# Reordering the prologue of a spectral-filter and MLP kernel: warm-up matmuls, first table group, filter loads and last product pair

## The chip, the cores and the metric

The kernel runs on one core of one Trainium2 chip. The metric is device microseconds of one execution, smaller is better. The profile's "span" is the time from the first to the last instruction of one profiled execution; the measured time was 2.1 to 2.2 us longer than the span of the same execution in runs of the kernel before. Engines are written TensorE (PE in profile lines), VectorE (DVE), ScalarE (ACT), GpSimd (POOL) and SyncE (SP). L107 is line 107 of that kernel's source, so the same statement has another number in another version.

Unless it is called a single look, a result below is six runs in the fast state, of which one was profiled. A single look is one run, whose state is unknown.

## The reference

```python
# x (8, 3008, 256), filt_r and filt_i (1505, 256), w_in (256, 2048), w_out (2048, 256), beta (2048)
X = np.fft.rfft(x, axis=1)
y = np.fft.irfft(X * (filt_r + 1j * filt_i)[None], n=3008, axis=1)   # the mixing
t = y.reshape(8 * 3008, 256)
h = t @ w_in
g = h * (1.0 / (1.0 + np.exp(-beta * h)))
out = g @ w_out
```

The kernel computes the transforms as matmuls with sine and cosine tables that it makes on the chip, in a 47 x 64 factorization.

## The kernel before

The first batch item's mixing has to be finished before the MLP can start, and nothing else can fill TensorE meanwhile. This is the prologue. From then on the MLP loop runs, and the mixing of the other seven items is woven into it. The prologue's steps are:

1. Load x of item 0 in six transfers and make the tables: the first in `t1b`, the second, `t2`, from angles `u` and `r` on VectorE (first half) and GpSimd (second half), a sine on ScalarE, and three copies (`t2_more`).
2. First stage (`first1`, eight groups), evicted to `a_t`.
3. Turns: `a_t` transposed into `a2`.
4. Twelve products: second-stage matmuls, evicted by VectorE with a multiplication by the filter `fri`, two per product (`pb_t`, `qb_t`).
5. The inverse (`inverse3`) with tables `t3`, `t3b`, which are transposes of `t2` (`table3`), to `z_t`; then turns of z, the last stage to `y`, and the loop.

The filters come in three groups, `FG`: products 1 to 3 use group 0, products 4 to 6 use group 1, and products 7 to 12 use group 2. The "lower" half of a filter is in long rows, the "upper" half in 1 KB rows. `held` is a tiny GpSimd read that keeps the large loads of `w_in`, `w_out` and the next x back until group 1's upper halves are there.

```python
    mark = dpool.tile([1, D], BF16, name="mark", tag="mark")
    nc.sync.dma_start(mark[:], x_cur[:1, JG, :])       # SyncE's queue waits here for x's third transfer
    ...
    FG = ((0, KG), (KG, KG), (2 * KG, 2 * KG))
    for h in range(2):
        for f, at in ((filt_r, 0), (filt_i, M)):
            load_filter(fri, f, at, *FG[0], gp)[h]()                 # group 0: GpSimd
    for h in (1, 0):
        for f, at in ((filt_r, 0), (filt_i, M)):
            load_filter(fri, f, at, *FG[1], nc.sync)[h]()            # group 1: SyncE
    for go in load_filter(fri, filt_r, 0, *FG[2], nc.sync):          # group 2, real part: SyncE
        go()
    ...
    warm(12)                                    # 12 matmuls on zeros, their result is not used
    ...                                         # angles, tables
    held = setup.tile([P, 1], F32, name="held", tag="held")
    for p0 in (H, M + H):
        gp.tensor_copy(held[p0 : p0 + H], fri[p0 : p0 + H, 2 * KG - 1, :1])
    load_win(0); load_win(1); load_wout(0) ...  # GpSimd's large loads, behind held (shortened)
    for i in range(2):
        first1(i, (True, True))
        warm(2)
    t2_part(0, 0)
    first1(2, (False, False))
    warm(2)
    for part in (1, 2):
        t2_part(0, part)
    for go in load_filter(fri, filt_i, M, *FG[2], nc.scalar):        # group 2, imaginary part: ScalarE
        go()
    for i in range(3, 5):
        first1(i, (False, False))
        warm(2)
    t2_more(0, nc.vector)                       # three table copies on VectorE
    first1(5, (True, True))
    ...
    turn_a(0, False)
    turn_a(1, True)
    ...
    table3(0, 2, True)
    product(0)
    table3(0, 0, False)                         # first table group, evicted between the products
    FLAG = 2
    for i in range(NK // 2 + FLAG):
        if 0 < i < NK // 2:
            product(i)
        ...                                     # further turns and table groups
        if i >= FLAG:
            inverse3(i - FLAG)
    for i in range(4):
        scale_wout(i)
    for at in (0, M):                           # frr, for the later items: SyncE's queue
        for go in load_filter(frr, filt_r, at, 0, JG, nc.sync):
            go()
```

## Time and profile before

Three runs before the prediction gave a median of 790.13 us (790.11 to 791.49). The execution that was profiled was a fourth one and took 792.89 us, with a span of 790.8 us. The mean granted TensorE clock of that execution was 0.997.

| what | value |
|---|---|
| time, median of 3 | 790.13 us |
| time and span of the profiled execution | 792.89 us, 790.8 us |
| first product on VectorE | 19.70 us |
| seventh product | 29.52 us |
| first matmul of the loop | 41.36 us |
| granted TensorE clock, 10 to 15 us | 0.66 |

From the profile page of before: the busy time of each engine, with its share of the span and its instructions, and the chain of work that ended last, by engine.

```profile
PE 772.1 (98%) x6001; PEld 548.0 (69%) x6097; DVE 395.7 (50%) x643; ACT 596.9 (75%) x920; POOL 144.6 (18%) x143
...
PE 92%; DVE 3%; issue 2%; POOL 2%; ACT 1%; DVEq 0%; ACTq 0%; POOLq 0%
```

The loop is TensorE's. The prologue is not, so its own timeline must be read. From the timeline of VectorE, before; the columns are start and duration in us, engine, line, operation, output and input, count, and in brackets the idle time before it and what ended that.

```profile
13.38 0.35 DVE L289 TENSOR_SCALAR t<-t 128x768 bf16<-128x768 bf16 x1
13.65 0.98 DVE L290 COPY t<-t 128x768 bf16<-128x768 bf16 x1
14.55 1.97 DVE L291 COPY t<-t 128x768 bf16<-128x768 bf16 x1
16.45 0.54 DVE L107 CAST a_t<-psa 128x384 bf16<-128x384 f32 x1
17.63 0.56 DVE L107 COPY a<-pb 128x768 bf16<-128x768 bf16 x1 [0.64 <-PE pb L409]
19.70 0.69 DVE L442 TENSOR_TENSOR pb_t<-ps,fri 128x512 bf16<-128x512 f32 x1 [1.52 <-DMA fri<-in_filt_i_dram]
...
29.52 0.68 DVE L442 TENSOR_TENSOR pb_t<-ps,fri 128x512 bf16<-128x512 f32 x1
```

The three copies (the first with a change of sign) are of one size and take 0.35, 0.98 and 1.97 us. The first product (19.70) was released by a filter's landing. The seventh (29.52) waited for nothing, and VectorE has no gap between the two: in this execution VectorE is what limits the products.

From the timeline of TensorE, the first matmul of the loop:

```profile
41.36 1.02 PE L791 MATMUL hps<-y,win_sb 128*128 128x512 bf16 x4 [0.35 <-DVE y L109]
```

### The profile page before, as it was taken

The numbers are of one execution on the slowest core, as the hardware profiler recorded it, in microseconds if no ns is written. First come the engines' busy times: TensorE is split into PE (matmuls) and PEld (weight loads), VectorE is DVE, ScalarE is ACT, GpSimd is POOL, SyncE is SP. The second block draws the span as 40 slices with busy tenths as digits, with TensorE's granted clock in tenths as the row PEclk, the third lists the DMA queues.
The fourth block names the chain that finished last, engine by engine and source line by source line (L and its number), as shares of the span: only waits on it lengthen the run. The fifth ranks groups of instructions, "written<-read, shape, count | busy, mean of one in ns | idle before, by whom it ended". The sixth has DMA issues, their size and how long they took to land.

```text
span 790.8 us, 15274 instructions
## 1 busy us (share of the span) xinstructions
PE 772.1 (98%) x6001; PEld 548.0 (69%) x6097; DVE 395.7 (50%) x643; ACT 596.9 (75%) x920; POOL 144.6 (18%) x143
## 2 busy tenths in 40 slices
PE   7899999999999999999999999999999999999998
PEld 4767667766677667776668766687667766776665
DVE  7946935755527464465634746367462760500101
ACT  5887886886678866788667876778767788677776
POOL 8421510430014200131002310024100340000000
PEclk9999999999999999999999999999999999999999
DMA  8978678116811178011860229402370214010101
GB/s 183 235 191 215 145 207 224 56 67 187 204 56 47 68 200 218 29 68 60 216 190 28 78 103 197 155 30 92 126 208 27 74 68 127 28 54 27 55 27 53
DMA packets 83379, 91.43 MB, mean 116 GB/s; under 512 B 3758, under 2 KB 73536, under 8 KB 82286
## 3 DMA queue, kind: packets, MB, share of 16 engines
q1 hardware_dynamic: 79756, 73.16, 30.0%
q0 software_dynamic: 2816, 16.26, 10.8%
q10 hardware_dynamic: 736, 1.05, 0.6%
q8 instruction: 47, 0.77, 0.4%
q14 instruction: 24, 0.20, 0.1%
HBM read 57.16 MB, written 46.66 MB: 131 GB/s over the span
## 4 chain that ended last, share of the span: by engine, by line
PE 92%; DVE 3%; issue 2%; POOL 2%; ACT 1%; DVEq 0%; ACTq 0%; POOLq 0%
PE acc L826 42%; PE hps L791 37%; PE ps L599 3%; PE ps L522 3%; PE ps L621 2%; PE ps L647 2%; DVE ost L107 1%; POOL xg L116 0%; POOL r L269 0%; DVE qb_t L442 0%; ACT a L105 0%; DVE pb_t L442 0%; PE pb L409 0%; PE psz L452 0%; DVE q_t L636 0%
## 5 line engine op out<-in xcount | busy, mean ns | idle before, releaser
L800 ACT ACTIVATE gT<-hps,beta_sb 128x512 bf16<-128x512 f32 x752 | 516.5, 687 | 175.8 <-PE hps L791 147.9
L826 PE MATMUL acc<-wout_sb,gT 128*128 128x256 bf16 x3008 | 455.1, 272 | 3.8 <-ACT ost L105 0.2
L791 PE MATMUL hps<-y,win_sb 128*128 128x512 bf16 (+7 forms) x1634 | 427.4, 350 | 0.3 <-DVE y L109 0.3
L826 PEld LDWEIGHTS <-gT 128*128 128x128 bf16 x3008 | 285.4, 98 | 132.6 <-issue 4.5
L791 PEld LDWEIGHTS <-win_sb 128*128 128x128 bf16 x1728 | 164.7, 98 | 24.8 <-issue 0.7
L637 POOL TENSOR_TENSOR v_t<-p_t,q_t 128x512 bf16<-128x512 f32 x84 | 106.7, 1270 | 376.3 <-DVE q_t L636 373.7
L107 DVE COPY ost<-acc 128x512 f32<-128x512 f32 (+1 forms) x88 | 56.2, 677 | 193.6 <-PE acc L826 188.0
L107 DVE CAST a<-ps 96x512 bf16<-96x512 f32 x96 | 65.9, 687 | 85.5 <-PE ps L599 85.4
L109 DVE TENSOR_SCALAR y<-ps 128x376 bf16<-128x376 f32 (+2 forms) x120 | 64.5, 541 | 64.4 <-PE ps L522 64.2
L632 DVE TENSOR_TENSOR p_t<-ps,frr 128x512 f32<-128x512 f32 x84 | 58.1, 691 | 31.8 <-PE ps L621 29.5
L636 DVE TENSOR_TENSOR q_t<-ps,fri 64x512 f32<-64x512 f32 x84 | 58.2, 693 | 1.2
L633 DVE SCALAR_TENSOR_TENSOR q_t<-ps,fri 64x512 f32<-64x512 f32 x84 | 57.4, 684 | 1.1
L522 PEld LDWEIGHTS <-zz 96*128 96x128 bf16 x512 | 35.3, 97 | 29.0
L105 ACT ACTIVATE z<-ps 128x512 bf16<-128x512 f32 x84 | 49.5, 589 | 0.7 <-PE ps L647 0.7
L599 PE MATMUL ps<-xg,t 94*96 94x512 bf16 x112 | 41.9, 381 | 0.8
L522 PE MATMUL ps<-t,zz 96*128 96x94 bf16 x448 | 36.7, 204 | 1.1
L116 POOL DMA_DIRECT2D xg<-in_x_dram x22 | 12.1, 556 | 114.3 <-PE acc L826 97.7
L647 PE MATMUL ps<-v_t,t 128*128 128x256 bf16 x168 | 32.1, 273 | 0.4 <-DVE q_t L636 0.4
L621 PE MATMUL ps<-a,t 128*128 128x256 bf16 x168 | 32.1, 273 | 0.4
L621 PEld LDWEIGHTS <-t 128*128 128x128 bf16 x168 | 15.8, 98 | 14.6
L599 PEld LDWEIGHTS <-t 94*96 94x96 bf16 x112 | 13.8, 123 | 12.1
L647 PEld LDWEIGHTS <-t 128*128 128x128 bf16 x168 | 15.4, 98 | 8.1 <-DVE q_t L636 0.9
(118 smaller groups left out, 196.9 us busy)
## 6 DMA issues: line engine op xcount, KB each, us to landing
out_dram<-ost SPq DMA_DIRECT2D x40, 512.0 KB, 2.8
d<-a SPq DMA_DIRECT2D x28, 384.0 KB, 3.5
a<-d SPq DMA_DIRECT2D x28, 384.0 KB, 5.2
d<-z SPq DMA_DIRECT2D x28, 384.0 KB, 2.6
zz<-d SPq DMA_DIRECT2D x28, 384.0 KB, 4.4
xg<-in_x_dram POOLq DMA_DIRECT2D x6, 1280.0 KB, 10.2
frr<-in_filt_r_dram SPq DMA_DIRECT2D x12, 256.0 KB, 6.8
out_dram<-ost SPq DMA_DIRECT2D x22, 128.0 KB, 9.0
```

What stands on the lines that cost most here:

```text
L107: nc.vector.tensor_copy(dst, src)
L109: nc.vector.tensor_scalar_mul(dst, src, scale)
L522: nc.tensor.matmul(ps[:, e, :NP], lhsT=zz[:, jj + e, dc * P : (dc + 1) * P], rhs=tab[:], start=True, stop=True,)
L599: nc.tensor.matmul(ps[:KP], lhsT=t1[:], rhs=s["x"][:, 2 * i : 2 * i + 2, :], start=True, stop=True)
L621: nc.tensor.matmul(ps[:, e, :], lhsT=t2[:, k0 + e, 3:5, :].rearrange("p c k -> p (c k)"), rhs=s["a2"][g][:, kk + e, :], start=True, stop=True,
L632: nc.vector.tensor_tensor(p_t[:], ps[:], frr[:, ks_, :], ALU.mult)
L636: nc.vector.tensor_tensor(q_t[:M], ps[M:P], fri[M:P, ks_, :], ALU.mult)
L637: nc.gpsimd.tensor_tensor(v_t[:], p_t[:], q_t[:], ALU.add)
L647: nc.tensor.matmul(ps[:, e, :], lhsT=t3[:, k0 + e, :], rhs=v_t[:, e, :], start=True, stop=True)
L791: nc.tensor.matmul(hps[:, pos - t0 : pos - t0 + ln], lhsT=win_sb[:, dc, fb * P : (fb + 1) * P], rhs=ys[b][:, dc, n0 : n0 + ln], start=(dc ...
L800: nc.scalar.activation(gT[:, :tn], hps[:, :tn], ACT.Silu, scale=beta_sb[:, fb : fb + 1])
L826: nc.tensor.matmul(acc[tb // per][:, tb % per, :], lhsT=gT[:, tb * P : (tb + 1) * P], rhs=wout_sb[:, fb, :], start=(fb == 0 and tb % per = ...
```

## The change

Its intent, in four parts:

- **Warm-ups.** More matmuls on zeros ahead of the third first-stage group (14 in place of 12 at the start, 8 in place of 2 later, and 1 in place of 2 before the last group), to keep TensorE's clock up while it waits for x.
- **First table group.** Its transposes are issued right behind the first stage and its evictions come before the first turn, so that they leave the stretch of products.
- **Filters.** Group 2 is loaded wholly on SyncE, in the order in which it is used, and no longer half on ScalarE. The `held` wait and GpSimd's large loads move behind the first stage in the program; some of those loads move to the fourth step.
- **Last pair.** Its two halves go to two PSUM banks and are evicted by ScalarE and VectorE at once.

The diff, cut to its core (cuts marked `...`; the moved code is not shown twice):

```diff
-    for go in load_filter(fri, filt_r, 0, *FG[2], nc.sync):
-        go()
+    for h in (0, 1):
+        for f, at in ((filt_r, 0), (filt_i, M)):
+            load_filter(fri, f, at, *FG[2], nc.sync)[h]()
...
-    warm(12)
+    warm(14)
...
     for i in range(2):
         first1(i, (True, True))
-        warm(2)
+        warm(2 if i == 0 else 8)
...
-    for go in load_filter(fri, filt_i, M, *FG[2], nc.scalar):
-        go()
...
     first1(7, (False, True))
+    tabs = [
+        table3(0, 0, False, fpsum.tile([P, KG, P], BF16, name="pt", tag="f")),
+        table3(0, 2, True, hpsum.tile([P, KG, P], BF16, name="pt", tag="hps")),
+    ]
+    for go in tabs:
+        go()
...
+    for p0 in (H, M + H):
+        gp.tensor_copy(held[p0 : p0 + H], fri[p0 : p0 + H, 2 * KG - 1, :1])
...
     turn_a(0, False)
     turn_a(1, True)
...
+        last = i == NK // 2 - 1
+        one = opsum.tile([P, 2, NDC, P], F32, name="psz", tag="acc")
+        two = fpsum.tile([P, 2, NDC, P], F32, name="psz", tag="f") if last else one
...
-    table3(0, 2, True)
     product(0)
-    table3(0, 0, False)
     FLAG = 2
+    TAB = (1, 2, 5, 6, 8, 9)
```

More of the change, by code (lines that the diff above doesn't have):

```diff
@@ L288, in t2_more @@
         ks_ = slice(h * NH, (h + 1) * NH)
-        eng.tensor_scalar_mul(t2[:, ks_, 4, :], t2[:, ks_, 1, :], -1.0)
+        nc.vector.tensor_scalar_mul(t2[:, ks_, 4, :], t2[:, ks_, 1, :], -1.0)
         eng.tensor_copy(t2[:, ks_, 3, :], t2[:, ks_, 2, :])
@@ L313 @@
     )
-    held = setup.tile([P, 1], F32, name="held", tag="held")
-    for p0 in (H, M + H):
-        gp.tensor_copy(held[p0 : p0 + H], fri[p0 : p0 + H, 2 * KG - 1, :1])
-    def load_win(h):
-        fs = slice(h * FF // 2, (h + 1) * FF // 2)
-        gp.dma_start(win_sb[:, :, fs], moe_w_in[:, fs].rearrange("(dc p) f -> p dc f", p=P))
-    load_win(0)
-    load_win(1)
-    load_wout(0)
-    xs = {}
-    if B > 1:
-        xs[1] = load_x(1, X_HALVES[:2])
-    load_wout(1)
-    if B > 1:
-        load_x(1, X_HALVES[2:], xs[1])
-        mark3 = dpool.tile([1, D], BF16, name="mark3", tag="mark3")
-        nc.sync.dma_start(mark3[:], xs[1][:1, J - 1, :])
-    load_wout(2)
-    load_wout(3)
     a_t = ypool.tile([P, NDC, NK, J, 4], BF16, name="a_t", tag="y")
@@ L367, with table3, go @@
         t2_part(0, part)
-    for go in load_filter(fri, filt_i, M, *FG[2], nc.scalar):
-        go()
+    def table3(i, part, on_act, own=None):
+        pt = own or opsum.tile([P, KG, P], BF16, name="pt", tag="acc")
+        for e in range(KG):
+            nc.tensor.transpose(
+                pt[:, e, :],
+                t2[:, KG * i + e, part : part + 2, :].rearrange("p c k -> p (c k)"),
+                ident[:],
+            )
+        dst = t3 if part else t3b
+        def go():
+            if i > 0:
+                evac(dst[:, KG * i : KG * i + KG, :], pt[:], on_act)
+                return
+            if part:
+                evac(dst[:, 0, :], pt[:, 0, :], on_act, 0.5)
+            else:
+                nc.vector.tensor_scalar_mul(dst[:, 0, :], pt[:, 0, :], keep[:])
+            evac(dst[:, 1:KG, :], pt[:, 1:KG, :], on_act)
+        return go
     for i in range(3, 5):
@@ L376 @@
     first1(6, (True, True))
-    warm(2)
+    warm(1)
     first1(7, (False, True))
-    def table3(i, part, on_act):
-        pt = opsum.tile([P, KG, P], BF16, name="pt", tag="acc")
-        for e in range(KG):
-            nc.tensor.transpose(
-                pt[:, e, :],
-                t2[:, KG * i + e, part : part + 2, :].rearrange("p c k -> p (c k)"),
-                ident[:],
-            )
-        dst = t3 if part else t3b
-        if i == 0:
-            if part:
-                evac(dst[:, 0, :], pt[:, 0, :], on_act, 0.5)
-            else:
-                nc.vector.tensor_scalar_mul(dst[:, 0, :], pt[:, 0, :], keep[:])
-            evac(dst[:, 1:KG, :], pt[:, 1:KG, :], on_act)
-        else:
-            evac(dst[:, KG * i : KG * i + KG, :], pt[:], on_act)
+    tabs = [
[4 more added lines that the diff above has]
+        go()
     a2s = []
@@ L414, in turn_a, with load_win @@
         evac(a2s[-1][:, 3 * (i % 2) : 3 * (i % 2) + 3, :], pb[:], on_act)
+    held = setup.tile([P, 1], F32, name="held", tag="held")
+    for p0 in (H, M + H):
+        gp.tensor_copy(held[p0 : p0 + H], fri[p0 : p0 + H, 2 * KG - 1, :1])
+    def load_win(h):
+        fs = slice(h * FF // 2, (h + 1) * FF // 2)
+        gp.dma_start(win_sb[:, :, fs], moe_w_in[:, fs].rearrange("(dc p) f -> p dc f", p=P))
+    load_win(0)
+    load_win(1)
+    load_wout(0)
+    xs = {}
+    if B > 1:
+        xs[1] = load_x(1, X_HALVES[:2])
     turn_a(0, False)
@@ L447, in inverse3 @@
         p_t, q_t = pq.pop(i)
-        ps = opsum.tile([P, 2, NDC, P], F32, name="psz", tag="acc")
-        for src, tab in ((p_t, t3), (q_t, t3b)):
-            for e in range(2):
+        last = i == NK // 2 - 1
+        one = opsum.tile([P, 2, NDC, P], F32, name="psz", tag="acc")
+        two = fpsum.tile([P, 2, NDC, P], F32, name="psz", tag="f") if last else one
+        for e, ps in ((0, one), (1, two)):
+            for src, tab in ((p_t, t3), (q_t, t3b)):
                 for dc in range(NDC):
@@ L455, in inverse3 @@
                         rhs=tab[:, k0 + e, :],
-                        start=src is p_t and dc == 0 and e == 0,
+                        start=src is p_t and dc == 0 and (e == 0 or last),
                         stop=src is q_t,
@@ L459, in inverse3 @@
                     )
-        evac(
-            z_t[:, :, :, 4 * k0 : 4 * k0 + 8].rearrange("p c j (e a) -> p e (c j) a", e=2),
-            ps.rearrange("p e c (j a) -> p e (c j) a", a=4),
-            True,
-        )
+        for e0, e1, ps in ((0, 1, one), (1, 2, two)) if last else ((0, 2, one),):
+            evac(
+                z_t[:, :, :, 4 * (k0 + e0) : 4 * (k0 + e1)].rearrange(
+                    "p c j (e a) -> p e (c j) a", a=4
+                ),
+                ps[:, e0:e1].rearrange("p e c (j a) -> p e (c j) a", a=4),
+                e0 == 0,
+            )
     def table4():
@@ L482 @@
             t2_part(1, i)
-        if i % 3 > 0 and i // 3 < 3:
-            table3(1 + i // 3, 4 - 2 * (i % 3), i % 3 == 1)
+        if i in TAB:
+            n = TAB.index(i)
+            table3(1 + n // 2, 2 - 2 * (n % 2), n % 2 == 0)()
         if i == 3:
             t2_more(1, nc.vector)
+            load_wout(1)
+            if B > 1:
+                load_x(1, X_HALVES[2:], xs[1])
+                mark3 = dpool.tile([1, D], BF16, name="mark3", tag="mark3")
+                nc.sync.dma_start(mark3[:], xs[1][:1, J - 1, :])
+            load_wout(2)
+            load_wout(3)
             bps = hpsum.tile([P, NFB], F32, name="bps", tag="hps")
```

## The prediction

> **What bounds the kernel.** From 41.4 us on, the block loop is TensorE: the page gives PE 772.1 us busy of 790.8 and puts 92% of the chain of waits on PE. Nothing of the change touches the loop. It touches the 41 us prologue (first stage, turns, 12 filter products, inverse), and a microsecond saved there should be one microsecond of span.
>
> The prologue's timeline: TensorE waits for x until 10.21 us and finishes the first stage at about 16.2 us, while VectorE copies table columns slowly (0.98 and 1.97 us, against 0.34 us for the same copies later) beside GpSimd's angle work, until 16.45 us. VectorE then idles 1.52 us and starts the products at 19.70 us, released by the landing of the first group's imaginary filter. From 19.7 to 37.2 us VectorE has no gap: 24 products at a pitch of 0.60 us, table evictions and copies. That is the limiting stage. The last pair then costs a ScalarE eviction (37.73 to 38.33 us) before the z turns start at 38.38 us.
>
> **Terms.**
> 1. Filters. The imaginary part of group 2 leaves the ScalarE queue, whose packets ran beside the last packets of group 0 and group 1 from 14.5 us. Group 0 should land near 17.5 us, and the products should start when the first turn is evicted, near 18.6 us: -1.0 us.
> 2. First table group. Its 12 transposes run when t2 is ready (16.45 us) and delay the turn by about 0.1 us; its VectorE eviction (0.60 us at the pitch) moves out of the limiting stage into the idle 1.52 us: -0.6 us.
> 3. Last pair: two half evictions on two engines, about 0.1 us gained after the later last matmul.
> 4. Warm-ups: the granted clock of 0.66 between 10 and 15 us should go to about 1.0. The Trainium skill, "TensorE: Matmul & The Clock Gate", Part 1, names sustained activity as what raises the clock; this trace agrees, the slow matmuls follow the 2.3 us wait. Worth about 0, because VectorE's table copies end the first stage.
> 5. The risk: group 2 is now all on one queue behind group 1, and the hold on the w_in loads (which waits for group 1's upper halves) opens near 19 us instead of 21.3 us. So w_in packets arrive near 21.4 us, while group 2 still has its small 1 KB packets to move. The seventh product needs group 2 at about 27.5 us (29.5 us less 2.0). Alone on the queue, group 2 would land near 27.4 us on the slowest engine. "DMA: Bandwidth & Descriptors", Arbitration, has the engines alternate between queues; in this trace 1 KB packets on the slowest engine ran almost undisturbed before w_in packets, so I expect a partial delay: a stall of 0 to 4 us, about +0.7 us on average.
>
> Sum: about -1.0 us net, from 790.1 to **789.0 us**, 8 in 10 between 787.6 and 791.4. Faster by over 2%: 0.005; within 2%: 0.98; slower: 0.015.
>
> **What would show it.** (1) First product at 18.5 to 18.9 us, with no DMA release. (2) Table evictions before the first turn's eviction. (3) Two z_t evictions at once at the end. (4) Clock near 1.0 in 10 to 15 us, with the first-stage matmuls shorter but the first turn still near 17.2 us. (5) Any gap of VectorE before the seventh product released by a filter DMA; without one the loop starts near 39.6 us, 1.7 us early.
>
> **What would make it wrong.** A long stall at the seventh product (group 2 landing after 30 us makes the kernel slower); ScalarE or PSUM buffers becoming the limit once VectorE has less; the time gained being lost where the loop first needs w_out or the second x.

## The result, and the profile after

A ratio is the mean time of one kernel's fast runs over that of the other's of the same rounds, so it is not quite the ratio of the medians that are quoted.

| | runs | median us | lowest to highest us |
|---|---|---|---|
| before, same job | 6 | 791.2 | 790.11 to 792.99 |
| after | 6 | 792.52 | 791.77 to 793.43 |

The ratio is 1.0017, 95% interval [1.0002, 1.0031]: the same within 2%, and if anything slower. The time was predicted at 789.0 us, between 787.6 and 791.4, and it lies outside.

The profiled execution of after (span 789.8 us) shows something else. From its page, busy time and the chain that ended last:

```profile
PE 776.7 (98%) x6104; PEld 547.6 (69%) x6104; DVE 396.3 (50%) x644; ACT 596.9 (76%) x920; POOL 144.6 (18%) x143
...
PE 93%; DVE 3%; POOL 2%; issue 1%; ACT 1%; DVEq 0%; ACTq 0%; POOLq 0%
```

From the timeline of VectorE, after:

```profile
13.64 0.98 DVE L291 COPY t<-t 128x768 bf16<-128x768 bf16 x1
14.55 1.97 DVE L292 COPY t<-t 128x768 bf16<-128x768 bf16 x1
16.43 0.55 DVE L107 CAST a_t<-psa 128x384 bf16<-128x384 f32 x1
17.27 0.28 DVE L366 TENSOR_SCALAR t3b<-pt,keep 128x128 bf16<-128x128 bf16 x1 [0.29 <-PE pt L352]
17.47 0.48 DVE L107 COPY t3b<-pt 128x640 bf16<-128x640 bf16 x1
17.87 0.55 DVE L107 COPY a<-pb 128x768 bf16<-128x768 bf16 x1
18.89 0.69 DVE L443 TENSOR_TENSOR pb_t<-ps,fri 128x512 bf16<-128x512 f32 x1 [0.47 <-PE ps L434]
...
27.98 0.69 DVE L443 TENSOR_TENSOR pb_t<-ps,fri 128x512 bf16<-128x512 f32 x1 [0.22 <-PE pb L396]
```

From the timeline of TensorE, after, the first matmul of the loop:

```profile
40.30 1.02 PE L805 MATMUL hps<-y,win_sb 128*128 128x512 bf16 x4 [0.35 <-DVE y L109]
```

Between these two traces nearly every step came as predicted: the first product at 18.89 us without a wait for a DMA, the table evictions at 17.27 and 17.47 us ahead of the first turn's, only 0.22 us of idle time before the seventh product, and the loop 1.06 us earlier (41.36 to 40.30). The loop took 745.30 us before and 745.42 us after (first to last matmul), and the span fell by 1.0 us. Yet the timed runs were not faster. Either the gain is given back outside the prologue, or these two executions don't stand for the timed ones.

### The profile page after: what moved, and what is told of

It reads as the page before. It is cut to its first block, busy times and chain, and to the rows that moved or that the text cites. A ratio compares the mean times of both kernels' runs of the same rounds, so it can differ in the third digit from the quotient of the medians.

```text
span 789.8 us, 15387 instructions
## 1 busy us (share of the span) xinstructions
PE 776.7 (98%) x6104; PEld 547.6 (69%) x6104; DVE 396.3 (50%) x644; ACT 596.9 (76%) x920; POOL 144.6 (18%) x143
## 4 chain that ended last, share of the span: by engine, by line
PE 93%; DVE 3%; POOL 2%; issue 1%; ACT 1%; DVEq 0%; ACTq 0%; POOLq 0%
PE acc L840 41%; PE hps L805 40%; PE ps L613 3%; PE ps L536 3%; PE ps L635 2%; PE ps L661 2%; DVE ost L107 1%; PE psz L456 1%; POOL xg L116 0%; POOL r L270 0%; ACT a L105 0%; DVE q_t L650 0%; DVE p_t L646 0%; DVE q_t L647 0%; PE pt L352 0%
## 5 line engine op out<-in xcount | busy, mean ns | idle before, releaser
L805 PE MATMUL hps<-y,win_sb 128*128 128x512 bf16 (+7 forms) x1728 | 447.7, 351 | 0.3 <-DVE y L109 0.3
```

The lines of the kernel that those rows point to most:

```text
L805: nc.tensor.matmul(hps[:, pos - t0 : pos - t0 + ln], lhsT=win_sb[:, dc, fb * P : (fb + 1) * P], rhs=ys[b][:, dc, n0 : n0 + ln], start=(dc ...
```

## The experiments

**Theory 1:** each execution is one of several, because the DMA's landings vary between executions; the change helps where x lands late, as in the two traces above, and harms where it lands early. **Rival 2:** the prologue's gain is real and is given back in the loop. **Rival 3:** the reordered filters stall the products. **Rival 4:** the table copies slowed beside GpSimd are the limit, and nothing in the filters matters. All runs gave correct results.

The recorded expectations use letters of their own. In e1 to e4, A says that the change really saves what the two traces show, and B that the profiled run of before was unusually slow and the change costs something. From e5 on, R is a race of the copies with GpSimd that a late x loses (here rival 4), S is the stall of group 2 (here rival 3), and e5's "Rival D" is x's landing itself, not rival 4. In e11 and e12, R says that x has only two states.

Landings in the tables below are read from the semaphore updates in the traces. "x" is the landing of the third and the sixth transfer of x. "g0" and "g2" are the landing of the last load of filter groups 0 and 2. Times are us from the span's start.

### Copies of both kernels (e1, e2; five rounds each)

No edit.

> A control: the kernel before, word for word, run as if it were a change. It shows what a difference of nothing looks like and, unlike the shared runs of before, gives the span of every run. Ratio to before 1.000 within 0.001. Theory A (the change really saves about 1.0 us of the span, as the two traces say, and the longer measured time is what surrounds the span or scatter between runs): the spans here lie near 790.5 us, about 1 us above those of the changed kernel. Theory B (the profiled run of before was an unusually slow one, and its usual span is about 788 us, so the change costs about 1.5 us somewhere that a single trace doesn't show): the spans here lie near 788 us. Loop start near 41.4 us in either case.

> A control: the changed kernel, word for word, again. Theory A: spans near 789.6 us, about 1 us below the copy of before, loop start near 40.3 us, and a measured time equal to or below before (ratio 0.9985 to 1.000). Theory B: ratio 1.0017 again, spans 1 us or more above the copy of before, though the loop starts at 40.3 us.

Measured: e1 792.23 us, ratio 1.0003 [0.9989, 1.0017]; e2 791.87 us (790.97 to 797.52), ratio 1.0009 [0.9986, 1.0031]. What matters is in the traces:

| trace | x third, sixth | g0 | product 1 | g2 | idle before product 7 | loop starts | span |
|---|---|---|---|---|---|---|---|
| before | 9.19, 13.43 | 19.5 | 19.70 | 27.4 | 0 | 41.36 | 790.8 |
| after | 9.65, 13.24 | 17.1 | 18.89 | 27.8 | 0.22 | 40.30 | 789.8 |
| e1 (before) | 8.04, 12.11 | 15.6 | 15.86 | 25.3 | 0 | 37.72 | 787.5 |
| e2 (after) | 7.60, 12.19 | 16.1 | 16.29 | 26.8 | 1.88 | 39.34 | 788.7 |

The same program, before, starts its loop 3.64 us earlier in e1 than in the first trace. In e1, from the timeline of VectorE:

```profile
12.55 0.35 DVE L289 TENSOR_SCALAR t<-t 128x768 bf16<-128x768 bf16 x1
12.81 0.35 DVE L290 COPY t<-t 128x768 bf16<-128x768 bf16 x1
13.08 0.35 DVE L291 COPY t<-t 128x768 bf16<-128x768 bf16 x1
...
15.86 0.69 DVE L442 TENSOR_TENSOR pb_t<-ps,fri 128x512 bf16<-128x512 f32 x1 [0.47 <-PE ps L433]
...
25.75 0.68 DVE L442 TENSOR_TENSOR pb_t<-ps,fri 128x512 bf16<-128x512 f32 x1
```

All three copies now take 0.35 us, the first product waits for no filter, and the seventh has no gap. There is nothing left here for the filter part of the change to gain. In e2, the same view:

```profile
24.46 0.68 DVE L443 TENSOR_TENSOR qb_t<-ps2q,fri 128x512 bf16<-128x512 f32 x1
27.02 0.69 DVE L443 TENSOR_TENSOR pb_t<-ps,fri 128x512 bf16<-128x512 f32 x1 [1.88 <-PE pb L396]
```

The view puts this wait on TensorE's `pb`, which had long been done; group 2 landed at 26.8 us, 0.2 us before the product. So with x early, after loses 1.62 us (37.72 to 39.34) where with x late it gains 1.06 us. This is what theory 1 says, though on one early trace of before. The sum can be read from where products start. Early, the first product comes 0.43 us later (15.86 to 16.29), the stretch from there to the last `qb_t` without its idle time is 0.69 us shorter (17.06 to 16.37, the table part's gain), and the stall adds 1.88 us: +1.62 us.

Both recorded theories were missed in part: e1's span is near theory B's 788 us, but its loop start is 3.6 us from the 41.4 us that was expected in either case.

Of the fourteen traces of the experiments, ten had x early (third transfer at 7.5 to 8.4 us), e3, e5 and e8 had it late (9.4 to 9.8 us), and e11 in between (8.66 us), so it isn't a matter of exactly two states. Nine of the ten early traces are of versions of after, while of the six traces of versions of before only e1 had x early: that the change itself moves x's landing is a rival that no run here tested. The filters follow x: SyncE's first filter load goes out 0.3 to 0.4 us after that third landing in all sixteen traces, since `mark` waits for it.

### Which part stalls the seventh product (e3, e4; five rounds each)

e3 is before with the filter part alone; e4 is after with the filter part undone:

```diff
# e3, in before
-    for go in load_filter(fri, filt_r, 0, *FG[2], nc.sync):
-        go()
+    for h in (0, 1):
+        for f, at in ((filt_r, 0), (filt_i, M)):
+            load_filter(fri, f, at, *FG[2], nc.sync)[h]()
...
-    for go in load_filter(fri, filt_i, M, *FG[2], nc.scalar):
-        go()
# e4, in after: the same hunks turned round
```

> Before with the filter part alone (all of group 2 on the SyncE queue, in order; nothing on ScalarE's). Theory A: first product near 18.8 us in place of 19.7 us, loop start about 0.5 to 0.9 us earlier, since the first table group's eviction is still in the limiting stage; span down by as much. Theory B with the filters as the culprit (the earlier w_in loads or the longer SyncE queue push something later): ratio above 1.001 though the loop starts early.

> The changed kernel with the old filter order (imaginary group 2 on ScalarE's queue). Theory A: first product again held by the filter at 19.7 us, loop start near 40.7 us (0.6 us from the table group and the last pair), span about 0.6 us below before. Theory B with the filters as the culprit: measured time falls back to or below before, ratio 0.999 to 1.000; if another part is the culprit the ratio stays near 1.002.

Measured: e3 791.82 us, 0.9994 [0.9982, 1.0006]; e4 791.09 us, 0.9996 [0.9979, 1.0013]. Neither time differs from before's, so the traces decide. e3's had x late (9.41 us): group 0 landed at 16.6 us in place of 19.5 us, and the first product came at 18.92 us in place of 19.70 us, as recorded theory A expected. Of those 0.78 us only 0.19 us reached the loop (41.17), since VectorE waited at other products later. e4's had x early (8.22 us), so it compares with e2. From its VectorE timeline:

```profile
25.57 0.68 DVE L444 TENSOR_TENSOR qb_t<-ps2q,fri 128x512 bf16<-128x512 f32 x1
26.17 0.68 DVE L444 TENSOR_TENSOR pb_t<-ps,fri 128x512 bf16<-128x512 f32 x1
```

With the old filters the seventh product has no gap, and group 2 landed at 25.8 us against 26.8 us in e2. The filter part is what makes the stall: rival 3 holds, but only with x early. e4's loop started at 38.48 us, 0.86 us before e2's and still 0.76 us after e1's. A part of that rest is a cost of the warm-ups: the granted clock rose only at 6.9 us there, the zero matmuls took longer, and the third first-stage group started at 9.87 us (9.38 us in e1) though its x had been there since 9.24 us. The 0.86 us did not reach the span (788.6 us, against 788.7 in e2), since e4's loop was 0.8 us longer, 746.04 us; that is rival 2.

### Table copies two evictions earlier (e5, e6; five rounds each)

On before and on after:

```diff
     for i in range(3, 5):
         first1(i, (False, False))
         warm(2)
-    t2_more(0, nc.vector)
+        if i == 3:
+            t2_more(0, nc.vector)
```

> Before, with VectorE's three table copies two evictions (0.96 us) earlier in its order, so that they end before about 13.5 us even when x lands late. Theory R (a race: the copies take 0.98 and 1.97 us in place of 0.35 us only when x's third transfer lands late, near 10.0 us, and pushes them past about 13.6 us, into GpSimd's angle subtraction; this is what makes the span of either kernel scatter by 1 to 3 us): all three copies take 0.35 us whatever the landing of x, the first turn starts before 15 us, the loop near 37.5 to 38.7 us, the span 787.3 to 788.5 us, and the ratio to before is 0.996 to 0.999. Rival D (the x landing itself, not the copies, sets the prologue): the copies stay slow or the loop start stays near 41 us when x lands near 10 us.

> The changed kernel with the same earlier copies. Theory R with stall S (group 2, all on one queue and beside w_in's packets, lands near 27 us, so the changed kernel waits at the seventh product whenever its first stage is quick): copies 0.35 us, first product near 16.5 us, a gap of 1.5 to 2.5 us before the seventh product, which starts near 27.0 us, loop near 39.3 us, span near 788.7 us: about 1.2 us slower than the same repair on before. Without S the gap is below 0.3 us, the loop starts near 37.2 us, ahead of before with the repair.

Measured: e5 791.62 us, 1.0001 [0.9986, 1.0016]; e6 793.02 us, 1.0021 [1.0001, 1.0041]. e5's trace had x late (9.40 us) and is the cleanest test of rival 4. From its VectorE timeline:

```profile
12.41 0.35 DVE L289 TENSOR_SCALAR t<-t 128x768 bf16<-128x768 bf16 x1
12.67 0.36 DVE L290 COPY t<-t 128x768 bf16<-128x768 bf16 x1
12.94 0.36 DVE L291 COPY t<-t 128x768 bf16<-128x768 bf16 x1
...
19.46 0.69 DVE L443 TENSOR_TENSOR pb_t<-ps,fri 128x512 bf16<-128x512 f32 x1 [2.99 <-PE ps L434]
```

The copies are fast, the first turn comes 1.7 us earlier than in before, and then VectorE waits 2.99 us: group 0 landed at 19.3 us. The loop starts at 41.32 us, as before's (41.36). So with x late, before is bound by group 0's landing, and rival 4 falls for it. The expected ratio (0.996 to 0.999) was missed; the recorded rival, that the loop stays near 41 us with x late, held. e6's trace had x early and again a gap before the seventh product (2.02 us, group 2 at 27.0 us). Its loop started at 41.15 us, because TensorE's clock was also halved from 36.8 to 40.2 us, on the z turns. No other trace shows that halving there, so what set it off is open. Of what was expected, the gap came and the loop start of 39.3 us did not.

### Hold the large loads longer (e7, e9; five rounds each)

e9 is after with the hold moved to group 2's lower halves; e7 is that plus e6's edit:

```diff
-    for p0 in (H, M + H):
-        gp.tensor_copy(held[p0 : p0 + H], fri[p0 : p0 + H, 2 * KG - 1, :1])
+    for p0 in (0, M):
+        gp.tensor_copy(held[p0 : p0 + H], fri[p0 : p0 + H, NK - 1, :1])
```

> As the last, with the hold on the w_in loads moved from group 1's upper halves to group 2's lower halves, so that w_in's packets come after most of group 2. Theory S: w_in issued near 23 us, group 2 lands near 25.5 to 26 us, the gap before the seventh product shrinks to 0.3 to 1 us, loop near 38.0 us, span near 787.5 us. If w_in's packets are not what delays group 2, it still lands near 27 us and the loop stays near 39.3 us. If the later loads then stall the loop (w_out, second x), the time from the loop's start to the last matmul grows above 745.7 us.

> The changed kernel with one edit: the hold on the w_in loads waits for group 2's lower halves in place of group 1's upper halves. Theory S (w_in's packets, let in too early, delay group 2 and so the seventh product): with x early (last x part near 12.1 us) group 2 lands near 25.6 us, the gap before the seventh product falls from 1.88 us to below 0.8 us, loop near 38.1 us; with x late (last part near 13.3 us) group 2 lands near 26.8 us in place of 27.8 us, the seventh product near 27.0 us, loop near 39.4 us. Rival (the queue's own length delays group 2, not w_in): group 2 at 27 us and later in either case, gap and loop as in the changed kernel.

Measured: e7 791.35 us, 1.0004 [0.9986, 1.0023]; e9 792.79 us, 1.0016 [0.9998, 1.0034]. In both, `w_in`'s load went out at 23.3 and 23.7 us in place of 18.7 us (e2). From e9's VectorE timeline:

```profile
24.49 0.68 DVE L443 TENSOR_TENSOR qb_t<-ps2q,fri 128x512 bf16<-128x512 f32 x1
25.97 0.69 DVE L443 TENSOR_TENSOR pb_t<-ps,fri 128x512 bf16<-128x512 f32 x1 [0.81 <-PE pt L352]
```

Group 2 landed at 25.8 us (e7: 25.6), a full 1.0 us before e2's, and the gap fell from 1.88 to 0.81 us (e7: 0.61). So a bit more than half of the stall is `w_in`'s packets beside group 2's last ones. e2's transfers show it: from 24 to 27 us SyncE's queue moved its last 46 packets (of 512 B or more) while GpSimd's moved 288. The other 0.6 to 0.8 us remain with group 2 having SyncE's queue to itself.

The loop now started at 38.10 us (e7) and 38.29 us (e9), 1.0 to 1.2 us before e2's. But it was longer: 746.43 and 746.87 us, against 745.24 us in e2. The times didn't fall. This is rival 2. Both traces already hold a wait of TensorE that neither first trace has, 0.78 us in e7 and 1.66 us in e9; from e9's timeline of TensorE:

```profile
53.79 0.33 PE L536 MATMUL ps<-t4b,zz 96*128 96x94 bf16 x4 [1.66 <-DVE a L107]
```

The next runs follow it.

### Copies away from GpSimd by moving GpSimd's work (e8; five rounds)

Before, with GpSimd's small operations on `m_p` and `keep` put behind both `angles`:

```diff
+    angles(0, nc.vector)
+    angles(1, gp)
+
     m_p = small("m_p")
     ...
-    angles(0, nc.vector)
-    angles(1, gp)
```

> Before, with GpSimd's angle work moved about 2 us earlier (its five small keep instructions after it, not ahead), so that its subtraction runs near 12.5 to 14.3 us. Theory R: now an early x makes the copies (12.5 to 13.5 us) collide: 0.9 us and up with x early, and a late x (13.4 to 14.4 us) collides for a short time only, ending near 14.9 us; the last first-stage eviction starts near 14.5 to 15 us in either case. Rival (the copies are slow because of the DMA traffic, the clock or x, not of GpSimd): copies 0.35 us with x early and slow with x late, as in before.

Measured: 791.0 us, 0.9996 [0.9981, 1.001]. The expectation was missed: GpSimd's angle work now came 2 us earlier and met VectorE's own angles. From the VectorE timelines, e8 and then before:

```profile
7.28 2.52 DVE L269 TENSOR_SCALAR r<-u 128x768 f32<-128x768 f32 x1
9.83 1.46 DVE L270 TENSOR_TENSOR u<-u,r 128x768 f32<-128x768 f32 x1
```

```profile
7.28 0.56 DVE L269 TENSOR_SCALAR r<-u 128x768 f32<-128x768 f32 x1
7.88 0.96 DVE L270 TENSOR_TENSOR u<-u,r 128x768 f32<-128x768 f32 x1
```

The contention moved and did not go. What slows the copies is confirmed all the same: in e8 they ran after GpSimd's subtraction had ended at 14.35 us, and were fast though x was late (9.77 us):

```profile
14.53 0.35 DVE L289 TENSOR_SCALAR t<-t 128x768 bf16<-128x768 bf16 x1
14.80 0.36 DVE L290 COPY t<-t 128x768 bf16<-128x768 bf16 x1
15.06 0.36 DVE L291 COPY t<-t 128x768 bf16<-128x768 bf16 x1
```

There was a second effect. The slower angles delayed ScalarE's sines, and with them its two group 2 loads, to 12.94 us (10.48 us in before). Group 0 then landed at 16.8 us in place of 19.5 us, the first product came at 18.44 us without a wait for it, and the loop at 40.31 us, as early as after's. With e3 this shows that ScalarE's loads are what makes group 0 late when x is late.

The Trainium skill, "SBUF — State Buffer", section "Who interferes with whom", says that VectorE and GpSimd share one pair of ports, which whoever comes first holds for its whole instruction. In before the copies agree: the two slow ones ended at 14.63 and 16.52 us, 0.2 us after GpSimd's rounding and its subtraction. e8 agrees less well: VectorE's rounding took 2.52 us in place of 0.56 us beside GpSimd's addition (7.88 to 9.37 us), although by the record VectorE's had started first. Times on GpSimd are rough in a profile.

### All mends together (e10; five rounds)

e10 is after with e7's two edits, fewer warm-ups and the table groups a step earlier:

```diff
-    warm(14)
+    warm(12)
-        warm(2 if i == 0 else 8)
+        warm(2 if i == 0 else 5)
-    TAB = (1, 2, 5, 6, 8, 9)
+    TAB = (1, 2, 4, 5, 7, 8)
```

> What the theories point to: the changed kernel with the hold on group 2's lower halves, the table copies two evictions earlier, the third table group turned one step earlier again (so that its eviction fills the wait for group 2), 12 and 5 warm-ups in place of 14 and 8. If the landing of group 2 is what bounds the prologue: the seventh product starts as it lands, near 25.7 us with x early and 26.9 us with x late, and the loop 11.9 us later: 37.6 or 38.8 us, against 37.7 or 41.4 us in before. Ratio to before 0.998 to 0.999. If loads for the loop are now too late: first matmul with w_out or the second x waits, and the loop's own 745.7 us grows.

Measured: 791.82 us, 0.9996 [0.9982, 1.0011]; a miss. The prologue did as hoped: no gap before the seventh product, loop start at 37.93 us. But the loop took 747.61 us, and the span was 789.6 us. So 2.3 us were lost inside the loop. From e10's timeline of VectorE and TensorE near 52 us:

```profile
52.84 1.28 DVE L107 CAST a<-ps 96x512 bf16<-96x512 f32 x2 [4.86 <-DMA d<-a]
...
53.58 0.33 PE L537 MATMUL ps<-t4b,zz 96*128 96x94 bf16 x4 [1.80 <-DVE a L107]
```

VectorE can't write the fourth `a` tile before the first one has been stored to `d` (there are three buffers). That store was issued at 45.5 us on SyncE's queue, behind the next item's mark and four `frr` filter loads issued from 43.6 us on. It landed at 52.7 us, and TensorE waited 1.80 us for VectorE. In e7 and e9 the same matmul waited (store landed at 51.9 and 52.9 us).

### Both kernels once more (e11, e12; single looks, state unknown)

No edit; with e9 and e10 on the same chip.

> Another look at the kernel before, to see whether its prologue has two states. Theory R: either x early (fourth x part near 9.3 us, group 0 near 15.7 us, loop near 37.7 us, span near 787.5 us) or x late (10.0, 19.5, 41.4, 790.8 us), nothing between by more than 1 us. Rival (continuous scatter): values between.

> Another look at the changed kernel. Theory R with S: x early gives a gap of 1.5 to 2.2 us before the seventh product and the loop near 39.3 us; x late gives a gap below 0.5 us and the loop near 40.3 us. Either way group 2 lands between 26.5 and 28 us, and the seventh product starts within 0.3 us of it.

Measured: e11 790.55 us, span 788.4 us, loop start 39.15 us; e12 792.21 us, span 789.8 us, loop start 39.02 us. e12 had x early (8.04 us) and the gap again (1.60 us, group 2 at 26.5 us). Its loop was 746.67 us long for yet another reason. From e12's timelines of GpSimd, VectorE and TensorE:

```profile
39.25 1.89 POOL L149 TENSOR_TENSOR wout_sb<-frr,rbeta_sb 128x1024 bf16<-128x1024 f32 x1 [3.90 <-DMA frr<-in_moe_w_out_dram]
...
39.38 2.58 DVE L586 TENSOR_SCALAR t<-t3b 64x3072 bf16<-64x3072 bf16 x1
...
42.73 0.38 PE L613 MATMUL ps<-xg,t 94*96 94x512 bf16 x1 [1.30 <-DVE a L107]
```

The negation of the third table (0.96 us where it runs undisturbed) started beside GpSimd's scaling of `w_out`, took 2.58 us, and cost TensorE 1.30 us.

### The loop's lost time taken away (e13, e14; five rounds each)

The cause of the first wait was open, so these two runs test it. e13 is e10 with the first four `frr` loads issued in the loop's step 7, after the second store; e14 is e13 with the last pair as in before (not shown) and the negation ahead of GpSimd's scaling:

```diff
# e13
-    for at in (0, M):
-        for go in load_filter(frr, filt_r, at, 0, JG, nc.sync):
-            go()
...
+        place(7, 7, uf((0,)), per=9)        # uf now takes the list of first rows
# e14
+    nc.vector.tensor_scalar_mul(t3[M:P], t3b[M:P], -1.0)
     for i in range(4):
         scale_wout(i)
...
-    nc.vector.tensor_scalar_mul(t3[M:P], t3b[M:P], -1.0)
```

> The last combination (e10) with one edit: the four loads of the first frr group are issued on SyncE after the second of the four stores of the second x's first stage, not before the first. If these loads are what makes the fourth tile wait (the first store landed at 52.7 us in e10, and TensorE waited 1.80 us there), the first store lands near 49 us, the wait is gone, and the time from loop start to last matmul falls from 747.6 to about 745.3 us; span 787.0 to 787.6 us with x early; ratio to before 0.996 to 0.998. Rival (all transfers share one full DMA backlog, so the order on the queue doesn't matter): the store still lands after 51.5 us and the wait stays above 1 us. If the loads are now too late for the filter products, VectorE waits for them near 68 us.

> The same, with the negation of the third table moved ahead of the z evictions (VectorE idles 1.3 us there, and GpSimd is idle), and the last pair in one bank again, since VectorE's half is in its way. Theory: the negation takes 0.96 us always, against 0.96 to 2.58 us in the traces so far; the loop starts near 38.1 us with x early, and the first w_out step comes 2.1 us after the loop's start instead of 2.5 us or more; span 786.8 to 787.5 us with x early, ratio to before 0.995 to 0.998. If the negation's wait for the last inverse matmul delays the z evictions, the loop starts 0.3 us or more later than in e13.

Measured, with before at a median of 792.34 us in the same job: e13 790.12 us (789.23 to 791.29), 0.9982 [0.9963, 1.0001]; e14 790.36 us (789.08 to 791.39), 0.9981 [0.9964, 0.9999]. From e13's timeline of VectorE and TensorE, the same tile and the same matmul as in e10:

```profile
49.70 0.69 DVE L107 CAST a<-ps 96x512 bf16<-96x512 f32 x1 [1.71 <-PE ps L610]
50.95 0.69 DVE L107 CAST a<-ps 96x512 bf16<-96x512 f32 x1 [0.56 <-PE ps L610]
...
51.62 0.33 PE L533 MATMUL ps<-t4b,zz 96*128 96x94 bf16 x4
```

The store landed at 46.9 us in place of 52.7 us, VectorE waits for TensorE and not for a DMA, and TensorE's wait is gone. The loop started at 37.93 us, exactly as in e10, and took 745.05 us in place of 747.61 us; the span is 787.1 us. Only the four loads' place differs, so the cause of the loop's lost time in e10 is shown. e14 (37.81 us, 745.06 us, span 787.0 us) adds 0.1 us, which no timing here resolves. Over all fast runs of the job, the spans of e13 and e14 average 788.1 us (12 runs, 787.0 to 789.3) and those of before 789.7 us (11 runs, 787.4 to 791.8). These versions beat before by some 0.2% in the same rounds (e13's interval just touches 1), and lie below after's two medians of other jobs, which ran on other chips (792.52 and 791.87 us).

So theory 1 stands for the traces, with rivals 2 and 3 inside it: with x early the filters stall the products (3), and where that stall is mended the loop gives back a part or all of what the prologue gains (2), until e13 removes that too. Rival 4 fell in e5.

## Why the prediction was wrong, point by point

- **The 41.36 us prologue as the kernel's own.** This is the step that failed. The prediction said that VectorE "starts the products at 19.70 us, released by the landing of the first group's imaginary filter", called the products "the limiting stage", and took -1.0 us and -0.6 us from that one execution. Over the three traces of before, the loop starts between 37.72 and 41.36 us and the first product between 15.86 and 19.70 us, as x and the filters land. Where they land early (e1), the 1.52 us wait that term 1 removes doesn't exist, and the landing of group 2, now all on one queue, sets the pace instead: the seventh product waited 1.88 us (e2). In e11, with x in between, the wait was still 1.43 us.
- **Term 1, filters (-1.0 us).** With x late, right: group 0 landed at 17.1 us (predicted near 17.5), the first product was at 18.89 us (near 18.6). With x early it turned into a loss.
- **Term 2, first table group (-0.6 us).** The evictions did move as predicted (17.27 and 17.47 us). With x late, the first product came 0.81 us earlier (term 1, predicted 1.0), the stretch from there to the last `qb_t` was 0.47 us shorter without its idle time (term 2, predicted 0.6), and the stall took 0.22 us: 1.06 us reached the loop. The seventh product came 1.54 us earlier (29.52 to 27.98), but one more table eviction now follows it, 0.48 us.
- **Term 3, last pair (-0.1 us).** It gave nothing. From the start of the last `qb_t` to the first z turn it took 1.82 us before (36.56 to 38.38) and 1.85 us after (35.50 to 37.35), for the two halves' eviction on two engines (0.39 and 0.42 us) started later.
- **Term 4, warm-ups (0).** The clock went from 0.66 to 1.00 in 10 to 15 us, as predicted, and it is worth nothing where VectorE or a landing ends the stage. The windows view of before and of after, for 10 to 15 us; the last three columns are clock, DMA share and GB/s:

```profile
10.00:15.00 5.00, 4.73 (x41) 3.10 (x43) 4.42 (x9) 2.44 (x5) 4.83 (x4) 0.66 1.04 245
```

```profile
10.00:15.00 5.00, 4.16 (x57) 2.83 (x57) 4.42 (x9) 3.59 (x8) 4.83 (x4) 1.00 1.03 237
```

  The Trainium skill, "TensorE: Matmul & The Clock Gate", Part 1, "What's actually happening", has the clock judged in a free-running window of about 3.4 us. The traces agree: half-clock stretches are 3.4 us long (11.6 to 15.0 us in before), and the first rise falls anywhere from 3.9 to 7.2 us in the same program's traces and its variants.
- **Term 5, the risk (+0.7 us on average).** The mechanism was right, the size was off: 0.22 us with x late, 1.88 and 1.60 us with x early. The prediction set the seventh product's need at 27.5 us and group 2's landing at 27.4 us. With x early the need comes at 25.1 us (e2), but the landing only at 26.8 us.
- **The base.** 789.0 is 790.13 less 1.1. The same job's six runs of before have a median of 791.2 us, and the 44 in the experiments' jobs a median of 792.12 us (789.51 to 793.97). So of the 3.5 us between 789.0 and 792.52, 1.1 us is a base of three lucky runs and 2.4 us is the change's own effect (predicted -1.1, measured +1.3 in medians; the interval of the ratio is 0.2 to 2.5 us, and e2's includes zero). The base and the timeline also came from different executions: the saving was read in one of 792.89 us and taken from a median of 790.13 us. Taken from 792.89 us it gives 791.8 us, against 792.25 us for after's profiled execution, which had x late too.
- **"A microsecond saved there should be one microsecond of span".** It held for the two first traces (1.06 us and 1.0 us) and nearly for e1 against the first trace (3.64 us and 3.3 us). It failed in e10, where 3.4 us bought 1.2 us of span, because a store behind four filter loads landed only at 52.7 us (51.2 us in e1, where TensorE waited 0.47 us). The prediction's last sentence guessed at such a loss, but at another place.

What came of it over many runs: spans of before average 789.75 us (44 fast runs, 787.4 to 791.8), those of after 790.17 us (12 fast runs, 788.6 to 795.2; 789.7 without the one of 795.2). Apart from that run, after has lost the fastest executions and the slowest ones alike, and the mean stayed (7 of before's 44 spans lie below after's lowest). This agrees with the traces (787.5 to 788.7 us with x early, 790.8 to 789.8 us with x late), but most of these executions left no trace, so it is argued and not shown.

One number for every run helps: the mean clock. One half-clock stretch of 3.41 us lowers it to 0.998 (half of 3.41 us is 0.2% of 790.8 us). Of before's 44 runs, 15 have 0.997 or 0.998, with spans of 790.2 to 791.4 us (mean 790.65); the other 29 average 789.29 us. The traces of before, e3 and e8 show such a stretch in the prologue, with x late; e5's has x late without one. So the execution that the prediction was read from belonged to the slower third, and its 0.997 was there to be seen.

Three things stay open. Why x lands early in one execution and late in another wasn't found; the loads are issued alike, and both kinds came up on one chip (e1 and e3, e5 and e7). After's time exceeded its span by 2.5 us on average (12 runs, 2.27 to 3.58) against before's 2.1 us, so 0.4 us of what was measured against it lies outside the span, where the trace shows nothing. And single runs of 794.4 to 797.5 us came up in e2, e4, e6, e7 and e9, all versions of after, and in none of before (highest 793.97 us in those 44); all of them had a mean clock of 0.997 or 0.998. e6's trace, another run with 0.998, shows a half-clock stretch on the z turns; none of the high runs left a trace.

## What to carry to other kernels

Read the time and the mean clock of the profiled execution beside those of the timed ones: if it is 2.8 us above their median, its waits are those of a slow execution, and terms as small as 1 us need a second and a third trace first. Before an early start is counted as gain, ask which transfer comes next in the same queue, and whether it is the later stage's bound whatever happens now; a store behind loads that nobody needs yet is such a place. When several waits end within one microsecond of each other, removing one only shows the next.

## What the Trainium skill lacked or had wrong

- "SBUF — State Buffer", "Who interferes with whom": it says that the one who comes second fully blocks until the first one's instruction ends. In e1 three VectorE copies ran from 12.55 to 13.43 us at 0.35 us each inside GpSimd's rounding operation `r` (11.71 to 14.52 us), and in before the copy that started at 13.65 us in the same operation (11.61 to 14.42 us) took 0.98 us. In e10 a copy that started at 11.74 us, just after that operation (11.72 us), took 1.02 us and the next two 0.35 us each. So there are stretches of a GpSimd instruction in which VectorE's copies pass; the page has none. The times on GpSimd are rough in a profile.
- "DMA: Bandwidth & Descriptors", "Queues, rings and completion order": the turns by packet between queues are borne out (99 packets of 512 B or more of SyncE's queue and 102 of ScalarE's between 22 and 23 us in before). The page has about 600 ns from issue to the first byte for a queue such as SyncE's ("Latency and other measured facts"), and nothing on how that grows beside another queue's backlog: SyncE's first filter load was issued at 9.5 us in before, and of its queue only `mark`'s one packet of 512 B moved before 13 us, while GpSimd's queue moved 44 to 54 such packets in each microsecond.
- No page tells how much the landing of the same load varies between executions of one program: the third transfer of x landed at 8.04, 8.66 and 9.19 us in three traces of before, and their loops started at 37.72, 39.15 and 41.36 us.
